# The load of the output weights moves behind three more scalings on GpSimd's queue

## The chip, the core and the metric

The kernel runs on one core of one Trainium2 chip. The metric is the device time of one execution in microseconds. The engines are named as in the profile: PE is TensorE, DVE VectorE, ACT ScalarE, POOL GpSimd, SP SyncE; an engine's instructions run in the order of its own queue, and a queue's order is fixed when the kernel is built.

## What is computed

```python
X = np.fft.fft(x, axis=1)        # x: (8, 3008, 256)
X = np.fft.fft(X, axis=2)
x = X.real.reshape(24064, 256)
g = x @ w_gate                   # (256, 1536)
silu = g * (1.0 / (1.0 + np.exp(-g)))
out = silu * (x @ w_val) @ w_out # (1536, 256)
```

The real part of a two-dimensional Fourier transform of each of 8 batches, and behind it a gated feed-forward block on all 24064 rows.

## The kernel before

**The transform.** Rows of x are loaded and folded on their symmetries, and the folded rows are multiplied with cosine and sine tables that the kernel makes itself. The transform along the 256 columns is not applied to x: it is put into the gate and value weights at the start, as Wp (even part) and Wq (odd part). Since the output has a mirror symmetry, only half of the rows are transformed. For each such column of the transformed x there is an even part Pt and an odd part Qt; the row itself takes Wp·Pt + Wq·Qt, and its mirror row Wp·Pt − Wq·Qt. In the first tiles the mirror is made by adding −2·Wq·Qt on top of the first sum, and the weights scaled so are Wm (partition 0 has the factor 0, the others −2, in the column m2).

**Tiles and units.** The columns are cut into tiles of 480 or 512; a tile has 12 units, one for each block of 128 hidden columns (`units`, L1297). A unit has matmuls for the gate and the value (L1346), a Silu on ACT, products on DVE or POOL into hp (rows) and hm (mirror rows). In the first tile ACT and DVE make these products (L1381, L1384, L1402, L1405); from the second tile on they go through sv, two buffers, which ACT (L1533) and DVE (L1549) fill and the product L1557 on POOL empties. The output matmuls (L1608, `OWork`) of a tile read hp, hm and the output weights Wo, are placed among the next tile's units, and ACT copies their sums out (L1614, L1617); SP stores them (L1620).

**The weights in the first tile.** The first 512 hidden columns of Wp, Wq and Wm are made before the first unit. The other four quarters (two blocks of 512, for gate and value) are made by `weight_op` (L1804) ahead of units 2, 3, 4 and 5: two products (L1814), a copy to Wp on DVE or ACT (L1817, L1820), a copy to Wq on ACT (L1823), and from that Wm on POOL (L1829, `mirrored_pool`). These four POOL instructions L1829 are the doublings of the change's name. Each waits for ACT's L1823.

**The output weights.** Wo is 1536 x 256, loaded from HBM by one DMA that POOL issues (L1980); it turns float32 into bfloat16 on its way.

**The loads of batch 1.** Rows of x come through SP's queue, in two sets. XC is the middle set: fifteen rising loads of 32 KB (L166), eight falling ones (L175), one middle row (L168), and at the end a copy inside the chip from one half of XC to the other (L180), which needs the rising loads landed. XA is the outer set: sixteen rising loads of 64 KB (L151) and four falling ones of 256 KB (L153 and its neighbours), which also wait for the last rising load of XC. SP uses eight semaphores in turn, so that a load is issued only when the one eight places ahead of it has landed. POOL folds first XC and then XA (L189 to L213, `fold_steps`); both stand in POOL's order among the products L1557.

**The order.** Operations are added to a planner (`Sched`, L1141) with engine, estimated time, what they read and write, and a wished place; `run` (L1184) plays them through on estimates and fixes each engine's order. The DMA of Wo is added as an operation of POOL with the time 1.06 us, and `lat`, the estimated time to landing behind it. Unit `i` of the main loop (L1956) adds it when `i` reaches the number in the condition at L1979.

Of the kernel before, what the change touches and what calls it, by code (L numbers as in the profile page):

```python
# [31 lines left out]
def kernel(  # L32
# [67 lines left out]
    Wm = const.tile([P, 2, Dff], BF16, name="Wm")  # L100
    Wo = const.tile([P, nF, D], BF16, name="Wo")
# [47 lines left out]
    def load_a(b, q):  # L149
        X3 = XA.rearrange("p a q d -> p a (q d)")  # L150
        res = ([lambda h=h: q.dma_start(out=X3[LA * h:LA * (h + 1), 0:4, :],  # L151
                                         in_=up_block(b, JA - LA * h, LA)) for h in range(NA)] +
                [lambda a=a: q.dma_start(out=X3[:, 4 + a, :], in_=down_set(b, a, JA, LA, NA)) for a in range(4)])  # L153
        return in_order(A1_ORDER, u=res[:NA], d=res[NA:]) if b == 1 else res
# [5 lines left out]
    def load_c(b, q):  # L160

        X3 = XC.rearrange("p a q d -> p a (q d)")
        p0 = 64 * (b % 2)
        pm = p0 + NCR
        r = slice(p0, p0 + NCR)
        ups = [lambda h=h: q.dma_start(out=X3[p0 + LC * h:p0 + LC * (h + 1), 0:4, :],  # L166
                                       in_=up_block(b, JC - LC * h, LC)) for h in range(NC_)]
        mid = [lambda: q.dma_start(out=XC[pm:pm + 1, 0:4, 1],  # L168
                                   in_=rows_at(b, 0, [[R * D, 1], [R * D, 4], [1, D]]))]
        if b != 1:  # L170
            return ups + [lambda a=a: q.dma_start(out=X3[r, 4 + a, :], in_=down_set(b, a, JC, LC, NC_))
                          for a in range(4)] + mid

        def down(a, k):
            q.dma_start(out=XC[0:NCR, 4 + a, 0] if k else XC[r, 4 + a, 0],  # L175
                        in_=rows_at(b, R * (a + 1) - 2 * JC + k, [[2 * LC * D, NC_], [-2 * D, LC], [1, D]]))

        downs = [[lambda a=a, k=k: down(a, k) for a in range(4)] for k in range(2)]
        return in_order(C1_ORDER, u=ups, d=downs[0], e=downs[1], m=mid,
                        c=[lambda: q.dma_start(out=XC[0:NCR, 0:4, 1], in_=XC[r, 0:4, 0])])  # L180
# [1154 lines left out]
    def seeded(u):  # L1335
        return kind(u) & 1
# [75 lines left out]
    def seed_op(u):  # L1412
        t, f = u
        w = width(t) + (B if t == nT - 1 else 0)
        kv = (("v", u), 0)

        def fn():
            T_[kv] = psV.tile([P, T], F32, name="v")
            nc.scalar.activation(T_[kv][:, :w], bc[t][:, :w], AF.Copy, scale=w0[:, 1, f:f + 1])  # L1419

        S.add("ACT", act_us(w) + 0.134, fn, r=[(("bc", t), 0)], w=[kv], new=[("v", u)], shift="SEED")
# [247 lines left out]
    def run_loads(n):  # L1669
        for what, k, fn in loads[:n]:  # L1670
            up = k < (NA if what[0] == "A" else NC_)
            r, w, us, ring = [], [((what[0],), k)], 0.4 if up else 0.62, 0.57 if up or what[0] == "C" else 1.14
            if what == ("A", 1):
                r = [(("C",), C1_ORDER.rindex("u"))]
                us, ring = (0.35, 0.5) if A1_ORDER[k] == "u" else (0.65, 0.9)
            if what == ("C", 1):
                us, ring = (0.35, 0.45) if C1_ORDER[k] == "u" else (0.85, 0.75)
                if C1_ORDER[k] == "c":
                    r = [(("C",), j) for j, o in enumerate(C1_ORDER) if o == "u"]
            S.add("SP", us, fn, r=r, w=w, after=[(("A",), "pre" if A1_ORDER[k] == "d" else "preW")] if what == ("A", 1) else [],  # L1680
                  lat=2.5, ring=ring)
        del loads[:n]
# [36 lines left out]
    def load_next(what):  # L1719
        kind, b = what  # L1720
        if kind == "A":
            if b + 1 < B:
                loads.extend((("A", b + 1), k, fn) for k, fn in enumerate(load_a(b + 1, nc.sync)))
        else:
            b = b // 2 * 2 + 2
            if b < B:
                loads.extend((("C", b), k, fn) for k, fn in enumerate(load_c(b, nc.sync) + load_c(b + 1, nc.sync)))
# [187 lines left out]
    def first_rows16(t):  # L1915
        w = row_width(t)

        def fn():
            T_["br", t] = brp.tile([P, T], BF16, name="br")
            nc.sync.dma_start(out=T_["br", t][0:P:8, :w], in_=pq_tiles(t)[1][0:1, :w].unsqueeze(1).to_broadcast([1, 16, w]))  # L1920
        return fn

    def all_rows(t):
        w = row_width(t)

        def fn():
            bc[t] = bcp.tile([P, T], BF16, name="bc")
            nc.sync.dma_start(out=bc[t][:, :w], in_=T_["br", t][0:P:8, :w].unsqueeze(1).to_broadcast([16, 8, w]))
        return fn

    def row_op(t):
        w = width(t)
        kr = (("g", ("bc", t)), 0)

        def product():
            T_[kr] = psG.tile([P, T], F32, name="g")
            nc.tensor.matmul(T_[kr][:, :w], sel, pq_tiles(t)[1][:, :w], start=True, stop=True)

        def copy():
            bc[t] = bcp.tile([P, T], BF16, name="bc")  # L1940
            nc.scalar.copy(bc[t][:, :w], T_[kr][:, :w])

        S.add("PE", pe_us(w), product, r=[(("pq", t), "Q")], w=[kr], new=[kr[0]])
        S.add("ACT", act_us(w), copy, r=[kr], w=[(("bc", t), 0)], new=[("bc", t)])
# [11 lines left out]
    for i, u in enumerate(units):  # L1956
        t, f = u
        S.tile = t
        for op in before.pop(i, ()):
            op()  # L1960
        if i == 1:
            loads.extend((("C", 1), k, fn) for k, fn in enumerate(load_c(1, nc.sync)))
        if i == A1_LOAD:
            loads[0:0] = ((("A", 1), k, fn) for k, fn in enumerate(load_a(1, nc.sync)))
        run_loads(LOADS if i < 20 else LOADS_LATER)
        if i in ROW_PE:
            row_op(ROW_PE[i])
        for j, k in enumerate((i - ROW_GAP, i)[::-1]):
            tr, fr = divmod(k, nF)
            if k >= 0 and fr == 6 and 2 < tr < nT - 1:  # L1970
                if j:
                    S.add("SP", 0.55, all_rows(tr + 1), r=[(("br", tr + 1), 0)], w=[(("bc", tr + 1), 0)], new=[("bc", tr + 1)], lat=4.5, shift="ROW")
                else:
                    S.add("SP", 0.55, first_rows16(tr + 1), r=[(("pq", tr + 1), "Q")], w=[(("br", tr + 1), 0)], new=[("br", tr + 1)], lat=3.6, shift="ROW")
        if i == RESCALE:
            state["scaled"] = True
            S.add("ACT", 1.3, lambda: nc.scalar.activation(Wm[:, 1], Wm[:, 1], AF.Copy, scale=-0.5),
                  r=[(("Wm",), (fc, 1)) for fc in range(3)], w=[(("Wm",), 1)])
        if i == 2:  # L1979
            S.add("POOL", 1.06, lambda: nc.gpsimd.dma_start(out=Wo, in_=moe_w_out.rearrange("(f p) d -> p f d", p=P)),  # L1980
                  w=[(("Wo",), 0)], lat=12.0)
        part_a(u)
        if owork:
            owork.run(4)
        if i + 1 < len(units) and seeded(units[i + 1]):
            seed_op(units[i + 1])
        if prev is not None:
            part_b(prev)
            if prev[1] == nF - 1:
                owork = OWork(prev[0])  # L1990
            if owork:
                owork.run(4)
        for what, j in fold_at.get(i, ()):
            fold_step(what, j, i)
        for what in act_at.pop(i, ()):
            load_next(what)
        if i in spread_at:
            spread_op(spread_at[i])
        if i in job_at:
            transform_op(*job_at[i])  # L2000
        prev = u
# [35 lines left out]
```

## Time and profile before

| | |
|---|---|
| time, median of 3 runs | 607.7 us (607.33 to 608.44) |
| profiled execution: its time | 607.87 us |
| profiled execution: span, first to last instruction | 606.1 us |
| busy: PE, DVE, ACT, POOL | 592.5, 571.4, 562.8, 509.7 us |
| granted TensorE clock, mean | 0.997 |
| DMA moved | 57.65 MB, mean 95 GB/s |
| Wo's DMA: issue, time to landing | 24.3 us, 9.2 us |
| first matmul that reads Wo | 39.7 us |

Times of day in the text are microseconds from the span's start. A profile view by groups gives the busy time of a group of instructions and the idle time of their engine just ahead of them, with who ended it. The chain of waits follows back from the last instruction to what released it, step by step. Windows give the busy time of each engine in a stretch, the clock that TensorE was granted (1.00 is full speed) and the share of the 16 DMA engines that was busy; where packets overlap, that share can pass 1. DMA queue q0 carries what POOL issues, q1 what SP issues.

### The profile page before, as it was taken

The numbers are of one execution on the slowest core, as the hardware profiler recorded it, in microseconds if no ns is written. First come the engines' busy times: TensorE is split into PE (matmuls) and PEld (weight loads), VectorE is DVE, ScalarE is ACT, GpSimd is POOL, SyncE is SP. The second block draws the span as 40 slices with busy tenths as digits, with TensorE's granted clock in tenths as the row PEclk, the third lists the DMA queues.
The fourth block names the chain that finished last, engine by engine and source line by source line (L and its number), as shares of the span: only waits on it lengthen the run. The fifth ranks groups of instructions, "written<-read, shape, count | busy, mean of one in ns | idle before, by whom it ended". The sixth has DMA issues, their size and how long they took to land.

```text
span 606.1 us, 12508 instructions
## 1 busy us (share of the span) xinstructions
PE 592.5 (98%) x3974; PEld 392.2 (65%) x4031; DVE 571.4 (94%) x1055; ACT 562.8 (93%) x1086; POOL 509.7 (84%) x460
## 2 busy tenths in 40 slices
PE   8999899999999999999999999999999999999997
PEld 5556566666666666666666666666666666666685
DVE  8989699999999999999999999999999999999993
ACT  8999798899989899999999999999999999999994
POOL 9737998999799999998999988887878467687772
PEclk9999899999999999999999999999999999999999
DMA  9846347254616214454136212036211112111112
GB/s 240 142 106 136 113 118 182 65 141 114 185 39 166 80 55 121 121 130 129 55 82 142 66 45 81 18 94 179 63 62 37 57 43 66 42 54 51 54 53 79
DMA packets 50555, 57.65 MB, mean 95 GB/s; under 512 B 7267, under 2 KB 37399, under 8 KB 50489
## 3 DMA queue, kind: packets, MB, share of 16 engines
q1 hardware_dynamic: 47529, 53.97, 32.8%
q0 software_dynamic: 2672, 2.36, 2.7%
q8 instruction: 31, 0.51, 0.4%
q10 hardware_dynamic: 288, 0.52, 0.3%
q14 instruction: 35, 0.29, 0.2%
HBM read 29.43 MB, written 24.65 MB: 89 GB/s over the span
## 4 chain that ended last, share of the span: by engine, by line
PE 88%; DMA 5%; ACT 2%; issue 1%; DVE 1%; POOL 1%; SPq 1%; DVEq 0%; ACTq 0%
PE o L1608 38%; PE g L1346 24%; PE v L1346 19%; DMA XA<-in_x_dram 3%; DMA XC<-in_x_dram 2%; PE g L1766 2%; PE o L1766 2%; PE v L1608 1%; PE o L1814 0%; POOL SDf L189 0%; ACT sp L1458 0%; PE o L605 0%; PE g L605 0%; POOL hm L1557 0%; ACT sv L1533 0%
## 5 line engine op out<-in xcount | busy, mean ns | idle before, releaser
L1557 POOL TENSOR_TENSOR hm<-sv 128x1024 bf16<-128x1024 f32 (+2 forms) x137 | 254.8, 1861 | 52.2 <-ACT sv L1533 24.0
L1549 DVE SCALAR_TENSOR_TENSOR sv<-es,v 128x512 f32<-128x512 f32 (+2 forms) x264 | 175.8, 670 | 9.3 <-PE v L1346 4.8
L1608 PE MATMUL o<-Wo,hm 128*128 128x256 bf16 (+1 forms) x1128 | 164.8, 274 | 0.4
L1560 DVE TENSOR_TENSOR hp<-sp,v 128x512 bf16<-128x512 f32 (+2 forms) x238 | 157.9, 670 | 5.0 <-PE v L1346 3.6
L1608 PE MATMUL o<-Wo,hp 128*128 128x256 bf16 (+1 forms) x1104 | 160.2, 272 | 0.7
L1608 PEld LDWEIGHTS <-hm 128*128 128x128 bf16 (+2 forms) x1140 | 112.6, 99 | 59.6 <-issue 3.3
L1608 PEld LDWEIGHTS <-hp 128*128 128x128 bf16 (+2 forms) x1140 | 111.9, 98 | 56.0 <-issue 1.8
L1533 ACT ACTIVATE sv<-g 128x512 f32<-128x512 f32 (+2 forms) x182 | 120.8, 678 | 5.6 <-POOL hm L1557 2.8
L1458 ACT ACTIVATE sp<-g 128x512 f32<-128x512 f32 (+2 forms) x182 | 113.5, 626 | 5.9 <-PE g L1346 3.2
L1346 PE MATMUL g<-Pt,Wp 128*128 128x512 bf16 (+2 forms) x282 | 105.8, 375 | 3.7 <-ACT sv L1533 2.7
L1419 ACT ACTIVATE v<-bc,w 128x512 f32<-128x512 bf16 (+2 forms) x146 | 105.4, 724 | 2.0 <-DVE sv L1549 1.0
L1346 PE MATMUL v<-Pt,Wp 128*128 128x512 bf16 (+2 forms) x287 | 105.3, 375 | 0.5
L1483 DVE SCALAR_TENSOR_TENSOR es<-bc,w,v 128x512 f32<-128x512 bf16 (+2 forms) x128 | 93.3, 732 | 2.7 <-PE v L1346 0.4
L1481 ACT ACTIVATE es<-v 128x512 f32<-128x512 f32 (+2 forms) x146 | 90.5, 622 | 5.6 <-DVE sv L1549 2.7
L1346 PE MATMUL g<-Qt,Wq 128*128 128x512 bf16 (+2 forms) x246 | 90.3, 374 | 0.3
L1346 PE MATMUL g<-Qt,Wm 128*128 128x512 bf16 (+2 forms) x192 | 72.1, 377 | 0.9 <-ACT sg L1381 0.5
L1346 PEld LDWEIGHTS <-Wp 128*128 128x128 bf16 x576 | 56.4, 98 | 25.1 <-issue 0.8
L1462 DVE SCALAR_TENSOR_TENSOR sg<-bc,w,g 128x512 f32<-128x512 bf16 (+2 forms) x92 | 66.2, 722 | 1.9 <-PE g L1346 1.5
L1533 ACT ACTIVATE sv<-sg 128x512 f32<-128x512 f32 (+2 forms) x92 | 64.0, 699 | 1.0 <-DVE sg L1526 0.9
L1530 ACT ACTIVATE sp<-g 128x512 f32<-128x512 f32 (+2 forms) x92 | 56.9, 618 | 5.3 <-DVE sg L1526 5.1
L1346 PEld LDWEIGHTS <-Wq 128*128 128x128 bf16 x430 | 42.0, 98 | 30.4 <-issue 6.4
L1526 DVE SCALAR_TENSOR_TENSOR sg<-sg,g 128x512 f32<-128x512 f32 (+2 forms) x92 | 60.7, 660 | 0.1
(196 smaller groups left out, 768.8 us busy)
## 6 DMA issues: line engine op xcount, KB each, us to landing
out_dram<-ev SPq DMA_DIRECT2D x96, 128.0 KB
XA<-in_x_dram SPq DMA_DIRECT2D x30, 256.0 KB
XA<-in_x_dram SPq DMA_DIRECT2D x112, 64.0 KB
XC<-in_x_dram SPq DMA_DIRECT2D x28, 120.0 KB
XC<-in_x_dram SPq DMA_DIRECT2D x105, 32.0 KB
bc<-br SPq DMA_DIRECT2D x19, 128.0 KB
St<-Fc SPq DMA_DIRECT2D x12, 128.5 KB
out_dram<-ev SPq DMA_DIRECT2D x12, 120.0 KB
```

Of the source, the lines that this page charges most:

```text
L1346: nc.tensor.matmul(ps[:, :n], Wt[:, gv, fs], src[:, :n], start=start, stop=stop, skip_group_check=True)
L1419: nc.scalar.activation(T_[kv][:, :w], bc[t][:, :w], AF.Copy, scale=w0[:, 1, f:f + 1])
L1458: nc.scalar.activation(sp_to()[:, :w], T_[kg][:, :w], AF.Silu)
L1462: nc.vector.scalar_tensor_tensor(T_[keg][:, :w], bc[t][:, :w], w0[:, 0, f:f + 1], T_[kg][:, :w], op0=Alu.mult, op1=Alu.add)
L1481: nc.scalar.activation(T_[kes][:, :w], T_[kv][:, :w], AF.Copy, scale=2.0 if on_pool(u) > 1 else 1.0)
L1483: nc.vector.scalar_tensor_tensor(T_[kes][:, :w], bc[t][:, :w], w0[:, 1, f:f + 1], T_[kv][:, :w], op0=Alu.mult, op1=Alu.add)
L1526: nc.vector.scalar_tensor_tensor(T_[kgm][:, :w], T_[keg][:, :w], 2.0, T_[kg][:, :w], op0=Alu.mult, op1=Alu.subtract)
L1533: nc.scalar.activation(sv()[:, f % 2, w - 1::-1, 1], T_[kgm if by_dve else kg][:, :w], AF.Silu)
L1549: nc.vector.scalar_tensor_tensor(sv()[:, f % 2, w - 1::-1, 0], T_[kes][:, :w], 2.0, T_[kv][:, :w], op0=Alu.mult, op1=Alu.subtract)
L1557: nc.gpsimd.tensor_tensor(hts_(t)[1][:, f - 1:f + 1, :w], sv()[:, :, :w, 1], sv()[:, :, :w, 0], op=Alu.mult)
L1560: nc.vector.tensor_tensor(hts_(t)[0][:, f, :wp], T_[ksp][:, :wp], T_[kv][:, :wp], op=Alu.mult)
L1608: nc.tensor.matmul(st["ps"][:n, j, :], hts[t][minus][:, f, c:c + n], Wo[:, f, :], start=(f == 0), stop=(f == nF - 1))
```

## The change

The operation that issues Wo's DMA is added at unit 7 rather than at unit 2. It is given a read of the last quarter of Wm, so that the planner puts it behind the last L1829, and its estimated landing is 6 us rather than 12.

```diff
-        if i == 2:
+        if i == 7:
             S.add("POOL", 1.06, lambda: nc.gpsimd.dma_start(out=Wo, in_=moe_w_out.rearrange("(f p) d -> p f d", p=P)),
-                  w=[(("Wo",), 0)], lat=12.0)
+                  r=[(("Wm",), (2, 1))], w=[(("Wo",), 0)], lat=6.0)
```

On the engines this is one move: on POOL, the DMA stood behind the first of the four L1829 and now stands behind the fourth. The orders of PE, DVE, ACT and SP are the same in both kernels, instruction for instruction.

## The prediction

> **What bounds the kernel now.** I read the page first (PE is busy 98% of the span, so only what makes TensorE wait, or lets its clock fall, can move the end), then TensorE's waits, then the chain of waits, then the one-microsecond windows around the one long wait. TensorE's waits after 60 us, in two answers (60 to 70, and 70 to the end):
>
> ```profile
> PE g L1346 <- ACT sv L1533: 2.7, 1, 2.7
> ```
> ```profile
> PE g L1346 <- ACT sp L1530: 0.7, 1, 0.7
> ```
>
> The columns are total, count, longest. One stall of 2.7 us and, in the 536 us behind it, 0.7 us. So whatever shifts the end of the long stall shifts the end of the kernel by nearly the same amount. The chain of waits says who ends it:
>
> ```profile
> 40.94 5.10 DMA XA<-in_x_dram
> 46.06 7.09 DMA XA<-in_x_dram
> ...
> 58.59 2.35 POOL SDf L189
> ...
> 62.11 1.09 POOL EOf L196
> 63.20 1.86 POOL hm L1557
> 65.08 0.69 DVE sv L1549
> ```
>
> Rows are start, duration, work. POOL's fold of batch 1 (L189) starts at 58.59, when the last row load into XA (L151, L153) has landed; POOL had been idle for 4.03 us ahead of it. Behind it in POOL's order stand two products L1557, which free the sv buffers; ScalarE's L1533 waits 2.84 us for that, and TensorE waits for ScalarE. From the fold's start to TensorE's restart at 65.77 is 7.2 us of fixed work. The XA loads set the stall.
>
> The stall also costs clock, in the windows (columns: stretch, length, busy of PE, PEld, DVE, ACT, POOL with counts, then granted clock, DMA share, GB/s):
>
> ```profile
> 65.00:66.00 1.00, 0.23 (x2) 0.11 (x2) 0.92 (x2) 0.77 (x2) 1.00 (x2) 1.00 0.27 76
> 66.00:67.00 1.00, 0.94 (x5) 0.43 (x4) 1.00 (x3) 0.95 (x2) 1.00 (x2) 0.75 0.47 121
> 67.00:68.00 1.00, 1.00 (x5) 0.69 (x4) 0.89 (x2) 0.94 (x2) 1.00 (x2) 0.50 0.51 158
> 68.00:69.00 1.00, 1.00 (x5) 0.71 (x4) 1.00 (x3) 1.00 (x3) 1.00 (x2) 0.50 0.46 148
> 69.00:70.00 1.00, 1.00 (x6) 0.70 (x5) 0.63 (x3) 0.78 (x2) 0.92 (x4) 0.55 0.53 158
> ```
>
> Lost are 0.25 + 0.50 + 0.50 + 0.45 = 1.7 us, right behind the only long stall after the start. A stall that goes would return up to 2.7 + 1.7 = 4.4 us; one that grows costs its growth alone. [...]
>
> **The change part by part.** Nothing is added or removed. The listing of both kernels shows one instruction moved on POOL, past three scalings L1829, and the other engines unchanged.
>
> *POOL's time.* The timeline of POOL:
>
> ```profile
> 24.34 1.11 POOL L1980 DMA_DIRECT2D Wo<-in_moe_w_out_dram  x1
> 26.50 0.72 POOL L1829 TENSOR_SCALAR Wm<-Wq,m 128x512 bf16<-128x512 bf16 x1 [1.04 <-ACT Wq L1823]
> 27.89 0.69 POOL L1829 TENSOR_SCALAR Wm<-Wq,m 128x512 bf16<-128x512 bf16 x1 [0.67 <-ACT Wq L1823]
> 30.56 0.69 POOL L1829 TENSOR_SCALAR Wm<-Wq,m 128x512 bf16<-128x512 bf16 x1 [1.98 <-ACT Wq L1823]
> ```
>
> The three scalings that the issue is moved past wait for ScalarE anyway (1.04, 0.67, 1.98 us), so they start no earlier: gain 0. The issue moves from 24.34 to about 31.2. The three memsets behind it (L1885, L1886, L1909, from 31.19 to 33.5) start 1.1 us later; POOL then idles 9.54 us until 43.05, which hides it. Without that cover it would be 1.1 us. The wait that the edit asks for is on POOL's own last scaling, which is ahead in order anyway: 0.
>
> *Wo's landing.* It lands 9.2 us after its issue: 33.5 now, and 31.2 + 9.2 = 40.4 by that row. Without other loads held up on the same DMA engines, about 38.5 to 39: 1.8 us from issue to the first packet and some 5.5 us of packets in the trace. TensorE first reads Wo at 39.67. So TensorE waits between 0 and 0.8 us there; I take 0.2. Behind that waiting matmul stands all of TensorE's order, but the stall at 63 is set by POOL and not by TensorE, and its 2.7 us take up all of 0.8. Cost at the end: 0.
>
> *What the transfer blocks.* This is the term that counts. While Wo moves (q0, issued by POOL), SP's loads (q1) nearly stop. DMA queues from 27 to 30 us (packets, MB, share):
>
> ```profile
> q0 software_dynamic: 983, 0.50, 128.3%
> q1 hardware_dynamic: 23, 0.04, 3.8%
> ```
>
> SP issued six loads in that stretch. Now SP's timeline, where gaps and long rows are waits for a landing eight issues back:
>
> ```profile
> 29.63 0.64 SPq L168 DMA_DIRECT2D XC<-in_x_dram  x1
> 30.94 2.00 SPq L166 DMA_DIRECT2D XC<-in_x_dram  x2
> 33.29 0.89 SPq L175 DMA_DIRECT2D XC<-in_x_dram  x1
> ...
> 38.67 0.90 SPq L180 DMA_DIRECT2D XC<-XC  x1
> 39.74 1.51 SPq L151 DMA_DIRECT2D XA<-in_x_dram  x4
> ```
>
> From 30.27 to 33.29 SP loses 0.67 + 1.2 + 0.35 = 2.2 us to Wo. With Wo later that loss goes. Adding SP's own issue rows from 30.3 (a pair L166 0.81, one L175 0.88, a pair 0.81, one 0.88, then the last L166), the last rising load of XC is issued at about 33.8 rather than 36.00, a gain of 2.2 us. But XC<-XC (L180), and every XA load behind it, waits for that load to land. Before, it was issued at 36.00 and L180 went at 38.67: 2.7 us without Wo. After, it is issued 2.6 us behind Wo's issue, in the blocked stretch. The nearest row is the load issued at 27.02, 2.7 us behind Wo's issue, whose semaphore SP got back at 33.29: 6.3 us. By that row it lands at 33.8 + 6.3 = 40.1. From below: unblocked at 33.8 + 2.7 = 36.5. I take 39.8, close to the blocked row, a little under it because fewer loads queue around Wo this time. So L180 goes at 39.8 rather than 38.67: **+1.1 us**, with bounds -2.2 and +1.4, and +2 if Wo itself is slower in company.
>
> *What follows from it.* From 40 to 58 the XA loads run one behind the other: SP waits eight times on XA (4.3 us), and the sixteen 64 KB loads land some 0.8 us apart. That is throughput, so the whole series shifts by 1.1: the fold starts at 59.7, TensorE restarts at 66.9. The fold of XC on POOL (43.05 to 51.4) also comes about a microsecond later; the 4.03 us of idle POOL ahead of L189 take that up, or it would cost the same microsecond. The half clock stays: the idle stretch grows from 2.7 to 3.6 us.
>
> **Sum:** gain on SP 2.2, blocked landing -3.3, POOL 0, Wo's own wait 0, clock 0: +1.1 us on the profiled execution (607.87, span 606.1, so 607.2). The median shown is 607.7, 0.2 below that execution: 608.8.
>
> **The rivals.**
> 1. *Transfers share fairly, and the loads come earlier* (faster). DMA is nearly empty from 33 to 39 (q1's share there is 22%), so Wo would fill a hole. If SP's loads pass between Wo's packets, the last XC load lands at about 37, XA starts some 1.7 us earlier, the stall shrinks to 1.0, and from the point where the idle stretch no longer drops the clock the 1.7 us of half clock go too: 606.0 down to 604.3. Against it stand 23 packets of q1 beside 983. [...] Chance 0.18.
> 2. *A wash.* Landing and issue trade evenly (last XC load at 38.4 to 39), as Wo's last packets leave most engines 7.1 us behind the issue, 38.3. Time 607.4 to 608.1. That the move never reaches the stall is the same case. Chance 0.20.
> 3. *Slower still.* Wo and the blocked loads delay each other beyond 40.4: XA starts 2 to 2.5 us late, and TensorE waits 0.8 or more for Wo, still hidden. 609.7 to 610.2. It decides once the last XC load lands after 40.6. Chance 0.17.
> 4. *The forecast*, +0.4 to +1.9: 608.1 to 609.6. Chance 0.45.
>
> **How the numbers follow.** 0.2% is 1.2 us, about what a measurement of this kernel can tell from no change. The forecast's case lies a little more than half within it (0.25 same, 0.20 slower); with rival 2 that makes same 0.45, with rival 3 slower 0.37, and rival 1 faster 0.18. The other three cases hold 0.82 from 607.4 to 610.2, but each of their ends is good to a few tenths only, so some 0.05 of that falls outside; to leave out no more than a fifth the range reaches down to the mild end of rival 1: 606.0 to 610.3.
>
> **What would show it.** Right: Wo issued near 31.2; SP without gaps from 30.3 to 34; L180 near 39.8; L189 on XA near 59.7; TensorE's wait for L1533 near 3.6. Wrong: q1 keeps moving packets beside q0 from 33 to 38 (rival 1); L180 before 38.7; a wait for Wo at 39.7 of several microseconds, which would outgrow its cover; or a stall at 63 that no longer follows the XA loads. Engines' instruction fetches go through the same DMA engines; one that lands in Wo's stretch and stalls an engine would add a loss that I have not counted.

## The result, and the profile after

| | before | after |
|---|---|---|
| median (range), us | 607.9 (607.33 to 608.52), 8 runs | 609.97 (609.12 to 610.25), 8 runs |
| ratio of the two, 95% interval | | 1.0031 [1.002, 1.0041] |
| measured a second time (e1): median, us | 607.98, 33 runs | 609.36 (608.64 to 610.12), 11 runs |
| ratio, 95% interval | | 1.002 [1.0011, 1.0029] |
| profiled execution: time, span, us | 607.87, 606.1 | 609.12, 607.3 |

The changed kernel is slower, by 2.07 us between the medians of the first measuring and 1.38 us in the second; by the ratios it is 1.9 and 1.2 us. From here on a difference is that of the medians, and a bracket behind it is the ratio's interval in microseconds. The profiled execution of after is the fastest of its eight, and the two traces show 1.25 us of the difference.

The move itself, in POOL's timeline after (start, duration, line, operation, in brackets the idle time ahead and who ended it):

```profile
31.23 1.10 POOL L1980 DMA_DIRECT2D Wo<-in_moe_w_out_dram  x1
...
44.39 2.35 POOL L189 TENSOR_TENSOR SDf<-XC 128x1020 f32<-128x1020 f32 x1 [9.72 <-ACT sg L1402]
...
59.66 2.36 POOL L189 TENSOR_TENSOR SDf<-XA 128x1020 f32<-128x1020 f32 x1 [3.73 <-DMA XC<-in_x_dram]
```

The issue is at 31.23 rather than 24.34; the last scaling ahead of it starts at 30.59 (30.56 before). The fold of XC starts 1.34 us later than before (43.05), and POOL still idles 3.73 us ahead of the fold of XA, which itself starts 1.07 us later than before (58.59).

SP's timeline after:

```profile
33.06 0.88 SPq L175 DMA_DIRECT2D XC<-in_x_dram  x1
33.99 0.46 SPq L166 DMA_DIRECT2D XC<-in_x_dram  x1
34.50 1.75 SPq L175 DMA_DIRECT2D XC<-in_x_dram  x2
40.01 0.90 SPq L180 DMA_DIRECT2D XC<-XC  x1
```

The gaps from 30 to 33 are gone: the last rising load leaves at 33.99 instead of 36.00. Then SP has nothing to issue that is allowed to go, until L180 at 40.01. SP's waits from 30 to 41 (total, count, longest) name what it waits for:

```profile
SPq L180 <- DMA XC<-in_x_dram: 3.6, 1, 3.6
```

and the DMA queues from 34 to 37 (packets, MB, share) say why that load takes 6 us:

```profile
q0 software_dynamic: 1001, 0.51, 127.8%
q1 hardware_dynamic: 31, 0.05, 5.6%
```

While Wo moves, q1 gets 31 packets through in 3 us; in the same stretch of before, with Wo already landed, it moved 206. The chain of waits after carries the delay on:

```profile
33.99 5.96 DMA XC<-in_x_dram
...
42.28 5.05 DMA XA<-in_x_dram
47.35 6.86 DMA XA<-in_x_dram
54.22 5.14 DMA XA<-in_x_dram
...
59.66 2.36 POOL SDf L189
...
66.83 0.63 PE g L1346 x2
```

The chain is longer at its start than before (it reaches back through one XC load of 5.96 us) and nearly the same behind it: three stretches of row loads, the fold, TensorE at 66.83, 1.06 us later than before. From L180 to the fold it is 19.65 us rather than 19.92, so that 1.34 us at L180 became 1.07 us at the fold.

TensorE's waits from 35 to 70 after:

```profile
PE g L1346 <- ACT sv L1533: 2.5, 1, 2.5
PE o L1608 <- DMA Wo<-in_moe_w_out_dram: 0.8, 1, 0.8
...
```

The second line is new: Wo lands at 40.84, 9.6 us behind its issue, and the first output matmul waits 0.8 us for it. TensorE comes to the long stall later by about as much as the stall's end moves, so the stall is no longer than before (2.5 against 2.7 us).

### The profile page after: what moved, and what is told of

Its sections match the earlier page's. It is cut to its first block, busy times and chain, and to the rows that moved or that the text cites. A ratio compares the mean times of both kernels' runs of the same rounds, so it can differ in the third digit from the quotient of the medians.

```text
span 607.3 us, 12565 instructions
## 1 busy us (share of the span) xinstructions
PE 596.5 (98%) x4031; PEld 392.4 (65%) x4031; DVE 572.6 (94%) x1055; ACT 563.6 (93%) x1086; POOL 510.3 (84%) x460
## 4 chain that ended last, share of the span: by engine, by line
PE 87%; DMA 7%; SPq 2%; POOL 1%; ACT 1%; issue 1%; DVE 0%; POOLq 0%; ACTq 0%; DVEq 0%
PE o L1608 38%; PE g L1346 25%; PE v L1346 18%; DMA XA<-in_x_dram 4%; DMA XC<-in_x_dram 3%; PE g L1766 2%; PE o L1766 2%; PE v L1608 1%; SPq L175 1%; SPq L166 1%; POOL EOA L511 0%; POOL SDf L189 0%; PE g L605 0%; PE o L605 0%; DVE SA L453 0%
## 5 line engine op out<-in xcount | busy, mean ns | idle before, releaser
L1608 PEld LDWEIGHTS <-hm 128*128 128x128 bf16 (+2 forms) x1140 | 112.4, 99 | 59.7 <-issue 3.4
L1533 ACT ACTIVATE sv<-g 128x512 f32<-128x512 f32 (+2 forms) x182 | 120.9, 679 | 5.5 <-POOL hm L1557 2.9
L1458 ACT ACTIVATE sp<-g 128x512 f32<-128x512 f32 (+2 forms) x182 | 113.6, 627 | 5.9 <-PE g L1346 3.7
L1346 PE MATMUL g<-Pt,Wp 128*128 128x512 bf16 (+2 forms) x288 | 108.0, 375 | 3.3 <-ACT sv L1533 2.5
L1346 PE MATMUL g<-Qt,Wq 128*128 128x512 bf16 (+2 forms) x288 | 105.9, 375 | 0.0
L1346 PE MATMUL g<-Qt,Wm 128*128 128x512 bf16 (+2 forms) x196 | 73.6, 377 | 0.5 <-ACT sg L1381 0.5
L1533 ACT ACTIVATE sv<-sg 128x512 f32<-128x512 f32 (+2 forms) x92 | 63.9, 699 | 1.0 <-DVE sg L1526 0.9
```

Source lines behind the costliest of these rows:

```text
L1346: nc.tensor.matmul(ps[:, :n], Wt[:, gv, fs], src[:, :n], start=start, stop=stop, skip_group_check=True)
L1458: nc.scalar.activation(sp_to()[:, :w], T_[kg][:, :w], AF.Silu)
L1533: nc.scalar.activation(sv()[:, f % 2, w - 1::-1, 1], T_[kgm if by_dve else kg][:, :w], AF.Silu)
L1608: nc.tensor.matmul(st["ps"][:n, j, :], hts[t][minus][:, f, c:c + n], Wo[:, f, :], start=(f == 0), stop=(f == nF - 1))
```

## The experiments

Two theories stood. **A:** Wo holds up SP's last rising load, so L180, the XA series and POOL's fold of XA come later, and the end follows the fold. **B:** the loss is TensorE's own new wait for Wo. A third question came out of the prediction: is the half clock behind the stall worth 1.7 us? Medians are against the kernel before in the same set of runs; "fold" is the start of POOL's L189 on XA in the profiled execution.

| run | what | median, us | before, us | ratio [95%] | L180 | fold | span |
|---|---|---|---|---|---|---|---|
| before | | | | | 38.67 | 58.59 | 606.1 |
| after | | 609.97 | 607.9 | 1.0031 [1.002, 1.0041] | 40.01 | 59.66 | 607.3 |
| e1 | the changed kernel again | 609.36 | 607.98 | 1.002 [1.0011, 1.0029] | 40.69 | 60.04 | 608.0 |
| e2 | before, TensorE 0.87 us later | 608.32 | 607.98 | 1.0008 [0.9999, 1.0017] | 38.75 | 58.43 | 605.9 |
| e3 | after, L180 behind four XA loads | 607.76 | 607.98 | 0.9998 [0.9989, 1.0007] | 42.40 | 58.62 | 607.1 |
| e4 | before, stall filled with matmuls | 607.78 | 607.98 | 1.0 [0.9991, 1.0009] | 38.76 | 58.45 | 606.0 |
| e5 | Wo in halves | 607.83 | 608.07 | 0.9995 [0.9986, 1.0003] | 39.13 | 58.42 | 605.8 |
| e6 | Wo behind the third scaling | 608.53 | 608.07 | 1.001 [1.0001, 1.0018] | 40.27 | 59.32 | 607.0 |
| e7 | Wo in quarters | 606.63 | 608.07 | 0.9975 [0.9967, 0.9984] | 37.94 | 57.39 | 605.1 |
| e8 | before, L180 behind four XA loads | 608.36 | 608.07 | 1.001 [0.9999, 1.0021] | 40.42 | 60.75 | 609.5 |
| e9 | after, rising XC loads first | 606.58 | 608.2 | 0.9982 [0.996, 1.0003] | 36.29 | 56.62 | 604.2 |
| e10 | before, rising XC loads first | 608.62 | 608.2 | 1.0006 [0.9997, 1.0014] | 39.27 | 58.75 | 606.4 |
| e11 | quarters, rising XC loads first | 606.48 | 608.2 | 0.9971 [0.9957, 0.9985] | 40.00 | 59.14 | 607.5 |
| e12 | before, POOL 1.09 us more in the fold | 609.49 | 608.2 | 1.0023 [1.0013, 1.0034] | 39.68 | 59.05 | 607.8 |

**e1: the changed kernel again.** No edit.

> The changed kernel once more, for a second profile and its time beside the kernel before on the same chip. Theory A (the loads of XC that Wo blocks delay XA, the fold on POOL and so TensorE's restart): 1.2 to 2.1 us slower than before, TensorE's wait for ScalarE's L1533 again 2.5 us or more, L180 issued near 40.0. Theory B (TensorE's own 0.8 us wait for Wo is what reaches the end): 0.8 us slower, and the wait at 63 to 66 us shorter by 0.8 than in the kernel before.

Measured +1.4 us [0.7, 1.8]. L180 goes at 40.69, 0.7 us later than in the first trace of the same kernel, the fold starts at 60.04, 0.4 us later, and the span is 0.7 us longer; 0.3 us of that arose behind the fold, and the traces do not say where. TensorE's wait for Wo was 1.3 us here. So the landing of the blocked load differs by 0.7 us between executions; the mechanism is the same.

**e2: TensorE later, nothing else.** In the kernel before, the first output matmul is issued nine times.

```diff
-            nc.tensor.matmul(st["ps"][:n, j, :], hts[t][minus][:, f, c:c + n], Wo[:, f, :],
-                             start=(f == 0), stop=(f == nF - 1))
+            [nc.tensor.matmul(st["ps"][:n, j, :], hts[t][minus][:, f, c:c + n], Wo[:, f, :],
+                             start=(f == 0), stop=(f == nF - 1 or k > 0)) for k in range(8 if (t, minus, c, f) == (0, 0, 0, 0) else 0, -1, -1)]
```

> The kernel before, with the first output matmul of the first tile done nine times rather than once (the eight extra results are overwritten): TensorE alone is late by 8 x 0.108 = 0.87 us at 39.7, as by a wait for Wo, and no transfer moves. Theory A: the stall at 63 takes it up, 0.0 to +0.2 us; the stall shrinks from 2.7 to about 1.8. Theory B: +0.8 us.

Measured +0.3 us [-0.1, +1.0]. TensorE's waits from 35 to 70 in e2:

```profile
PE g L1346 <- ACT sv L1533: 1.4, 1, 1.4
...
```

The stall shrank from 2.7 to 1.4 us and the span did not grow (the trace is of e2's fastest execution, 607.64): time taken from TensorE ahead of the stall comes out of the stall. The upper end of the interval alone would still let theory B have its 0.9 us; e3 and e9 decide that.

**e3 and e8: the copy L180 no longer ahead of the XA loads.** L180 is issued behind the first four XA loads, in the kernel after (e3) and in the kernel before (e8).

```diff
-            loads.extend((("C", 1), k, fn) for k, fn in enumerate(load_c(1, nc.sync)))
+            loads.extend((("C", 1), k, fn) for k, fn in enumerate(load_c(1, nc.sync))); copy_c, loads[-2] = loads[-2][2], (*loads[-2][:2], lambda: None)
...
-            loads[0:0] = ((("A", 1), k, fn) for k, fn in enumerate(load_a(1, nc.sync)))
+            loads[0:0] = ((("A", 1), k, fn if k != 3 else lambda fn=fn: [fn(), copy_c()]) for k, fn in enumerate(load_a(1, nc.sync)))
```

> The changed kernel, with SP's copy XC<-XC (L180) put behind the first four rising loads of XA instead of ahead of them; Wo stays late and TensorE's wait for it stays. Theory A: XA's loads no longer stand behind a copy that waits for a blocked load, the XA series comes 1.5 to 2 us earlier, the fold starts near 58 rather than 59.7, and the kernel gains 1.3 to 2.0 us on the changed one (it comes back to about the time before). Theory B: no gain on the changed kernel, still about 2 us slower than before.

> The kernel before (Wo early) with SP's copy L180 behind the first four rising loads of XA. Theory A: XA's loads start near 38.3 rather than 39.7, but the copy lands later, so the fold of XC starts near 45 rather than 43.1 and POOL reaches the fold of XA only near 56.6 at best (11.5 us from fold to fold in the run with the copy behind XA's loads); the fold of XA at 57.2 to 58, 0.5 to 1.3 us faster than before. Theory B: no change.

e3 takes the whole loss away: 607.76, in the same set of runs in which e1 gave 609.36. Its fold is at 58.62, as in the kernel before. XA's loads do not wait for the last rising XC load by themselves: that load was issued at 35.05, and when its landing lets L180 go at 42.40, four XA loads have left. Three of them waited 3.1 us in all for XC loads eight places ahead, so Wo still held them up, but the first left at 37.50 rather than 41.08. TensorE's waits from 40 to 606 in e3:

```profile
PE o L1608 <- DMA Wo<-in_moe_w_out_dram: 2.6, 1, 2.6
PE v L1346 <- ACT v L1419: 0.7, 1, 0.7
...
```

TensorE waits 2.6 us for Wo, three times as long as after, and the median is 1.6 us lower. **Theory B falls** as the cause of the loss. That does not make the wait for Wo free: in e3 the stall at 63 is gone, and the chain of waits, followed back from the last instruction, goes from Wo's landing at 42.8 over TensorE and no longer passes the fold. TensorE pays 2.6 us at Wo in place of 2.7 us at the stall. (The trace is of e3's slowest execution, 608.89; the second line, a wait near 414, is in neither kernel of the case, and its 0.7 us would account for most of what keeps the span, 607.1, so near to after's; no run separates that.) e8 missed: +0.3 us [-0.1, +1.3] instead of a gain. Its trace is of its slowest execution (611.25; median 608.36), with the fold at 60.75, so it does not show where the expected half microsecond went; that stays open.

**e4: the stall filled.** In the kernel before, 18 matmuls with no use run in the stall.

```diff
+            [nc.tensor.matmul(st["ps"][:n, 1, :], hts[t][1][:, f, c:c + n], Wo[:, f, :], start=True, stop=True) for _ in range(18) if (t, minus, c, f) == (0, 1, 2 * P, nF - 1)]
```

> The kernel before, with 18 extra matmuls of 256 columns (1.9 us) in TensorE's order just ahead of the matmul that stalls from 63.1 to 65.8 (their results are overwritten). They fill most of the stall, so the clock should stay full. If the half clock behind the stall costs what its window shows: 1.0 to 1.7 us faster. If it costs nothing at the end (POOL or ScalarE would have held TensorE anyway): 0.0 to 0.3 either way.

The windows in e4 (stretch, length, busy of PE, PEld, DVE, ACT, POOL with counts, then granted clock, DMA share, GB/s):

```profile
66.00:67.00 1.00, 0.95 (x8) 0.61 (x6) 1.00 (x3) 0.89 (x3) 1.00 (x2) 1.00 0.59 130
67.00:68.00 1.00, 1.00 (x8) 0.71 (x7) 0.89 (x2) 1.00 (x3) 1.00 (x2) 1.00 0.48 131
```

The clock stays at 1.00 where it was 0.75 and 0.50 before, and the time is the same: -0.2 us [-0.5, +0.5]. The fifth busy column is POOL: 1.00 in both windows, before (the prediction's windows) as here. POOL's next long wait behind the fold, in the kernel before:

```profile
58.59 2.35 POOL L189 TENSOR_TENSOR SDf<-XA 128x1020 f32<-128x1020 f32 x1 [4.03 <-DMA XC<-in_x_dram]
...
93.27 1.89 POOL L1557 TENSOR_TENSOR hm<-sv 128x1024 bf16<-128x1024 f32 x1 [2.33 <-DVE sv L1549]
```

From the fold to the product at 93.27 it is 34.68 us, with waits of 0.59 (at 89.04) and 2.33 us near the end of it and none ahead of them. In e4 the same two starts are 58.45 and 93.03: 34.58. After: 59.66 and 94.25: 34.59. That stretch has one length whether TensorE runs at half clock in it or not, since the sv buffers that TensorE's results go through come free at POOL's pace. In e4 TensorE idles again between 80 and 92, 0.4 us for L1533 and 0.3 us for L1458, where before it does not. The chain of waits agrees: in e4 it runs over POOL's work from 77.7 to 88.2, as it does for some 10 us in e1 and e2, whose clock also stayed at 1.00; in the kernel before it has no work of POOL behind 65.1. So at half clock TensorE takes about as long for that stretch as POOL does, and speeding up TensorE alone gains nothing.

**e12: POOL later, nothing else.** In the kernel before, one instruction of POOL's fold of XA (L193, 1.09 us) runs twice.

```diff
-            queue[what, q][j]()
+            [queue[what, q][j]() for _ in range(2 if (what, q, j) == (("A", 1), 0, 1) else 1)]
```

> The kernel before with one instruction L193 of POOL's fold of XA done twice (1.09 us more on POOL right behind the fold's start, same result; no DMA and no other engine touched). If POOL's stretch from the fold's start on sets the end, as the runs so far say: 0.9 to 1.2 us slower. If TensorE has slack enough behind its stall, or its own 0.8 us is what counts: under 0.3 us.

Measured +1.3 us [0.8, 2.1] for 1.09 us of POOL. Together with e2 and e4 this shows theory A's last step: a microsecond of POOL in that fold costs about a microsecond, while 0.87 us of TensorE ahead of it showed as 0.3 and a faster TensorE behind it gained nothing.

**e5, e6 and e7: other places and sizes for Wo.** e6 puts the whole transfer behind the third scaling; e5 puts one half behind the first and one behind the last; e7 puts a quarter behind each of the four. The cut is on the 12 blocks of Wo; the orders of the other engines are those of before. e7:

```diff
-        if i == 2:
-            S.add("POOL", 1.06, lambda: nc.gpsimd.dma_start(out=Wo, in_=moe_w_out.rearrange("(f p) d -> p f d", p=P)),
-                  w=[(("Wo",), 0)], lat=12.0)
+        if i in {2: (0, 3), 3: (3, 6), 6: (6, 9), 7: (9, 12)}:
+            S.add("POOL", 1.06, lambda a={2: (0, 3), 3: (3, 6), 6: (6, 9), 7: (9, 12)}[i]: nc.gpsimd.dma_start(out=Wo[:, a[0]:a[1]], in_=moe_w_out.rearrange("(f p) d -> p f d", p=P)[:, a[0]:a[1]]),
+                  r=[(("Wm",), {2: (1, 0), 3: (1, 1), 6: (2, 0), 7: (2, 1)}[i])], w=[(("Wo",), 0)], lat=6.0)
```

e5 is the same with `{2: (0, 6), 7: (6, 12)}`, e6 is the changed kernel with `i == 6` and `(("Wm",), (2, 0))`.

> Wo in two halves: hidden blocks 0 to 5 by one DMA at the old place (behind the first scaling), blocks 6 to 11 by a second at the new place (behind the fourth). Each blocks SP's loads for about 2.8 us instead of 5.5. Theory A, with POOL's fold of XA as the point that sets the end: SP has no long gap, the last XC load is issued near 33.9 and lands near 37, L180 near 37.2 rather than 38.7 (before) and 40.0 (changed), the fold of XA starts near 57.1, and the kernel is 1.0 to 1.8 us faster than before. Theory B (only TensorE's wait for Wo counts): no wait for Wo, so the time of before, within 0.3.

> All of Wo in one DMA behind the third scaling, issued near 28.6, landing near 37.8, so TensorE has no wait for it. Theory A: the last XC load is issued into Wo's tail and lands near 37.5 to 38.8; L180 between 37.5 and 38.9; time 1.2 us faster to 0.3 slower than before. A rule that later is worse at any place would give some 0.8 us slower than before (two thirds of the change's cost).

> Wo in four quarters, one behind each scaling. Theory A: like the halves, each block only 1.4 us long, but three quarters are still under way or over before the last XC load is issued at 33.9; L180 near 36.9 to 37.3; 1.0 to 1.8 us faster than before. Against it: three more issues on POOL (0.7 to 1.1 us each) between the scalings, where POOL waits for ScalarE 0.7 to 2.1 us anyway. Theory B: the time of before.

e7 came out as expected in its time, -1.4 us [-2.0, -1.0], with the fold at 57.39; L180 went at 37.94, 0.6 us behind what was expected. e6 cost 0.5 us [0.1, 1.1] and missed in its path: issued at 28.56, Wo took 11.5 us to land, TensorE waited 0.2 us for it, and L180 went at 40.27. Its time alone does not rule out that a later place is worse at any place; e9 below does, with Wo as late as after. e5 missed: -0.2 us [-0.9, +0.2]. SP's timeline in e5 shows why:

```profile
30.07 0.64 SPq L168 DMA_DIRECT2D XC<-in_x_dram  x1
31.78 0.60 SPq L166 DMA_DIRECT2D XC<-in_x_dram  x2
...
35.12 0.46 SPq L166 DMA_DIRECT2D XC<-in_x_dram  x1
...
39.13 0.90 SPq L180 DMA_DIRECT2D XC<-XC  x1
```

The first half still blocked a load that SP needed back (a gap of 1.07 us ahead of 31.78), so the last rising load left at 35.12, later than after, and then ran into the second half. The queues in e5 from 28 to 29, and in e7 from 32 to 35:

```profile
q0 software_dynamic: 389, 0.20, 145.9%
```
```profile
q0 software_dynamic: 600, 0.29, 77.3%
q1 hardware_dynamic: 136, 0.17, 20.8%
```

e5's microsecond has no packet of q1 at all (the same microsecond of before has 2 beside 377); in e7 q1 gets 136 through. In quarter microseconds, q0 is at full flow in four of e7's twelve, with 80 to 87 packets each, and q1 gets 22 packets beside these 332; in the other eight it gets 114 beside 268. So e7's loads passed mostly in the pauses between the quarters, and within a quarter they were held up as by the whole of Wo. The counts are what the traces show (q1 beside q0: 31 beside 1001 after, 0 beside 389 in e5, 22 beside 332 in e7's full flow); by what rule an engine chooses between the two queues they do not show.

**e9, e10 and e11: the rising XC loads first.** SP's last nine XC loads are put in another order, the five rising ones ahead of the four falling ones, after (e9), before (e10) and with Wo in quarters (e11).

```diff
-        return in_order(C1_ORDER, u=ups, d=downs[0], e=downs[1], m=mid,
+        return in_order("uuduuduuduuduumuuuuueeece", u=ups, d=downs[0], e=downs[1], m=mid,
```

> The changed kernel, with only SP's own order of XC loads altered: behind the middle row L168 the five last rising loads go first and the four falling ones behind them (the copy L180 keeps its place). Wo stays late, TensorE's wait for Wo stays. Theory A: the last rising load is issued near 32.2 rather than 34.0, lands before Wo's tail, near 36.5, L180 goes near 37 to 38.6 rather than 40.0, the fold of XA starts near 57.3 to 58.5, and the kernel gains 1.0 to 2.2 us on the changed kernel (about 607.2 to 608.4). Theory B (TensorE's wait for Wo): no gain, 609.4 to 610.

> The same order of XC loads in the kernel before. Theory A: the last rising load no longer holds up L180, which then follows from SP's own issue time, 38.2 to 38.4 rather than 38.7: 0.3 to 0.5 us faster. Theory B: no change.

> Wo in four quarters and the rising loads first, together. Theory A: the last rising load is issued near 33 and lands near 36.3; L180 near 37 (SP's own time), rather than 37.9 with the quarters alone; fold of XA near 56.4; 1.8 to 2.6 us faster than before. Against it: TensorE then arrives at its wait at 63 with almost no stall left, so the gain ends there. Theory B: the time of before.

SP's timeline in e9, and TensorE's wait there:

```profile
30.68 1.85 SPq L166 DMA_DIRECT2D XC<-in_x_dram  x5
32.58 3.54 SPq L175 DMA_DIRECT2D XC<-in_x_dram  x4
36.29 0.88 SPq L180 DMA_DIRECT2D XC<-XC  x1
```
```profile
PE o L1608 <- DMA Wo<-in_moe_w_out_dram: 1.4, 1, 1.4
```

The five rising loads leave ahead of Wo's first packets, L180 goes at 36.29 instead of 40.01, the fold is at 56.62 instead of 59.66, and the span is 3.1 us shorter than after: the same late Wo, with the wait for it longer than after, and faster than before in the median (-1.6 us [-2.4, +0.2]). The gain is larger than was expected. Its times spread from 604.88 to 612.68, and the interval reaches +0.2 us, so it is shown that the loss is gone and not that this version beats the kernel before. As in e3, the stall at 63 is gone, and the chain of waits goes over Wo's landing, at 41.9, TensorE and, from 75.8 to 86.3, POOL's products; the XA loads and the start of the fold no longer set the end there. e10 missed, +0.4 us [-0.2, +0.9]: there the same loads were held up by Wo from 30 to 35, and L180 went at 39.27. e11, -1.7 us [-2.6, -0.9], falls a little short of its expectation and adds nothing measurable to e7; its trace is of its slowest execution, 609.28, with L180 at 40.00.

## Why the prediction came out as it did

The direction was right, and so was the path by which it came; the forecast was 608.8 us, the median 609.97. That median is inside the stated range, 606.0 to 610.3, but above the forecast's own case (608.1 to 609.6) and at the times of rival 3, while the landing in the trace was the forecast's.

- **SP's gain of 2.2 us:** the last rising load left at 33.99, 2.0 us earlier. Right.
- **The blocked landing:** predicted 39.8 for L180, measured 40.01 (40.69 in e1). The row of the load issued at 27.02 gave 40.1 and was the better number; the step down from it was not earned.
- **The series behind it:** fold 59.7, measured 59.66; TensorE's restart 66.9, measured 66.83. So +1.1 us was forecast on the profiled execution and 1.25 came. That the fold agrees so well is in part luck: L180 was 0.2 us later than taken, and the series from it to the fold 0.3 us shorter. That the whole series shifts by the same amount holds only roughly: L180 went 2.02 us (e1) and 1.60 us (e6) later than before, and the fold 1.45 and 0.73 us. Why the series shortens is open.
- **The median:** 1.2 us above the forecast. Of that 0.2 is the median of before, 607.9 over eight runs against 607.7 over three. Of the 2.07 us between the medians the first trace, of after's fastest execution, shows 1.25; e1's trace, of an execution of 609.77 us, has a span 1.9 us above that of before, 1.45 of it at the fold. The term that the traces show mis-sized is the landing of the blocked load, 0.2 us (after) and 0.9 us (e1) later than taken. It does not make up the rest: at the fold only 0.0 and 0.3 us of it were left over the forecast, and some 0.4 us of e1's span arose behind the fold. What that is stays open. The second measuring, +1.4, is nearer the forecast; why the two differ is open too.
- **Wo's landing:** bounded by 38.5 and 40.4, with a wait of 0.2 us taken; it landed at 40.84, later than both, and the wait was 0.8, the upper bound. That Wo would go faster with fewer loads held up around it is not borne out: it took 9.6 us after and 9.9 in e1, against 9.2 before. The wait was hidden as argued (e2). TensorE came to the stall some 1.2 us later, 0.8 of it by this wait, so the stall stayed at 2.5 and did not grow to 3.6.
- **The premise that only TensorE's stall and clock can move the end:** wrong in its second half. "A stall that goes would return up to 2.7 + 1.7 = 4.4 us" does not hold: e4 gave the clock back (1.00 where it was 0.75 and 0.50) and gained nothing (-0.2 us [-0.5, +0.5]). The 1.7 us, what the windows from 66 to 70 lost of the clock, is an estimate of what TensorE's own work pays; here POOL's stretch behind the fold took it up (34.68 us before, 34.58 in e4). Rival 1 also took it that a shorter stall leaves the clock up; no run shows a length that decides it (0.50 behind 2.5 us after, 1.00 behind 2.7 us in e1). This did not touch the forecast, where the clock's term was 0, but it priced rival 1's far end, 604.3, wrongly.
- **Rival 1, transfers that share fairly:** refuted by 31 packets of q1 beside 1001 of q0 from 34 to 37. **Rival 2, a wash:** its last XC load at 38.4 to 39 did not occur; it came at 39.95. **Rival 3:** the landing stayed under its point of decision, 40.6, in the first trace, and passed it by some tenths at most in e1 (L180 at 40.69).
- **Instruction fetches, left uncounted:** they are the DMA queues of the kind instruction, 66 packets and 0.80 MB in the whole span before (q8 and q14). One packet of q8, 0.02 MB and 0.7% of the 16 engines, moved between 33 and 41 after; none of TensorE's waits from 35 to 70 is put down to it.

## What to carry to other kernels

A transfer is not free because the DMA engines are idle on average in the hole it is moved to (q1's share from 33 to 39 was 22% before, and the move cost 2.07 us): ask which load, issued just ahead of or into it, some engine is waiting for, and price that load at the landing time of a load that was already blocked so. Then cut the transfer into parts with pauses between them (e7, 1.4 us faster than before), or issue the awaited loads ahead of it (e9, 606.58 us, which took the loss away), rather than only moving it; and look next at who waits for the transfer itself, as TensorE does in e3 (2.6 us) and e9 (1.4 us). And an engine that is busy 98% of the span is not thereby the bound of each stretch: follow the stall to the engine that runs without a gap behind it, and price a change by that engine's time.

## What was not expected of the hardware

- The clock fell to 0.50 behind a stall of 2.5 us after and of 2.4 us in e11 (mean granted clock 0.997 in both), and stayed at 1.00 behind one of 2.7 us in e1 and of 2.4 us in e10 (mean 1.000 in both): in these runs a stall of this length dropped it in some and not in others. From the fold to the end it is 547.6 us after and 548.0 in e1, so the clock that was kept brought nothing there either.
- Wo's transfer as one DMA took 9.2 to 12.3 us from issue to landing, and both of these at the old place (before and e12); at the new place it took 9.6, 9.9, 11.2 and 10.2 us (after, e1, e3, e9).
